# Attention with a state, then a GELU layer: two transposes moved in the start-up of a one-core kernel

## The chip, the cores and the metric

The kernel runs on one core of a Trainium2 chip. The metric is the device time of one execution in microseconds (us); the median of several executions counts. A core has the engines TensorE (PE in the profile; PEld are its weight loads), VectorE (DVE), ScalarE (ACT) and GpSimd (POOL), and SyncE (SP), which here only issues DMAs. Each engine works through its own list of instructions in order and waits on semaphores for the others.

## What is computed

For each of 8 batches and 8 heads, x (512 x 64) and a small state (32 x 64) attend to each other; the results of all heads, put side by side, go through a layer with an exact GELU:

```python
scores = scale * np.matmul(x, state.transpose(0, 1, 3, 2))
a = np.exp(scores - scores.max(-1, keepdims=True))
a /= a.sum(-1, keepdims=True) + 1e-09
xread = np.matmul(a, state)                    # 512 rows a batch
scores2 = scale * np.matmul(state, x.transpose(0, 1, 3, 2))
a2 = softmax(scores2)                          # written out in the same way
sread = np.matmul(a2, x)                       # 32 rows a batch
y = concat([xread, sread], axis=2)             # 4352 rows of 512, heads side by side
h = y @ w_in                                   # 512 x 2048
g = 0.5 * h * (1.0 + erf(h / sqrt(2)))
return g @ w_out                               # 2048 x 512
```

## The kernel before

The order of all instructions is written out by hand. It works by batches. For batch b:

- `load_x` (L115) fetches x by a GpSimd DMA into one of two `xb` buffers. `rearr` (L221) copies it on GpSimd into `x4`, from which `xtr_dma` (L276) makes the transposed `xT` by a DMA transpose on SyncE's queue; batch 1 is transposed on TensorE instead (`xtr`). `rearr_ones` (L230) makes a second copy `xo` of the same x, with a column of ones; for batches 2 and up it runs on GpSimd (L235). `xo` is read by `sread` (L379) alone, the product for the 32 state rows.
- `scores` (L323) multiplies xT by the state and takes the exponential on ScalarE in two halves. `norm` (L345) does on VectorE, for each half, a sum (L351), a reciprocal (L353) and a scaling (L354), which gives A, the tile `a`.
- A must be transposed to A^T (`AT`). Batch 1 does this with `atr` (L361): eight TensorE transposes into two PSUM tiles `aT_ps` and two VectorE copies. Batches 2 and up use `atr_dma` (L371), a DMA transpose on SyncE's queue.
- The state times w_in gives P, in four chunks of 512 columns: `p_mm` makes two PSUM tiles, `p_copy` casts one on ScalarE (L433) and one on VectorE (L434). `burst` makes several chunks in one run; `pmat` makes one. In P the state and the first layer are folded together, so that `M(k)` (`mm1`, L478) makes one block of 128 of the 2048 hidden columns of a batch by two matmuls of A^T with P, and a GELU on ScalarE (L492). `M(16, 17)` are blocks 0 and 1 of batch 1.
- The second layer of batch 0 runs in units `mm2_m(0, m)` (L520): four matmuls that add hidden block m to all four row tiles of the output. From `U(12)` on, units run by row tile (`mm2`, L505). Later batches use sums of quarter matrices (`g_sum`, `X`), for which `w_sums` (L547) prepares sums of w_out on VectorE.

PSUM has two groups of buffers. `ps_f` is a ring of four that `ftile` gives out in program order; each of its tiles takes the buffer that the fourth tile before it had, and waits for that one's reader. `hp`, `p_ps`, `aT_ps`, `srT`, `pt` and `sr` go through this ring. `otile` gives out four others, which hold the running outputs.

A GpSimd instruction that copies one column into the tile `hold` (128 x 1) is used three times further on to make GpSimd's list wait: it reads a block of g, so that it, and the load behind it, can't start before the GELU of that block.

The order around the first part of the change, batch 0's second layer and batch 1's start, is the lines L1032 to L1045. Around the second part it is L1063 to L1090: the hold and load of batch 4, `rearr(3)`, `xtr_dma(3)`, `rearr_ones(3)`, batch 2's scores and norm, the sums of w_out, `atr_dma(2)` and `pmat(2, 3)`. After it comes the loop over batches 2 to 7, whose first product is `M(32, 33)` with batch 2's A^T.

Of the kernel before, what the change touches and what calls it, by code (L numbers as in the profile page):

```python
# [17 lines left out]
def kernel(  # L18
# [8 lines left out]
    nc = tc.nc  # L27
# [27 lines left out]
    def otile(shape, name, at=None):  # L55
        if at is None:
            at = turn[0] % 4
            turn[0] += 1
        return ps_o.tile(shape, FP32, name=name, tag=f"o{at}")
# [19 lines left out]
    hold = persist.tile([128, 1], BF16, name="hold")  # L79
# [124 lines left out]
    atts = {}  # L204
# [25 lines left out]
    def rearr_ones(b):  # L230
        A = atts[b]
        eng = nc.vector if b < 2 else nc.gpsimd
        src = xbs[b].rearrange("p (t c) (j d) -> p t c j d", t=2, d=D)
        for t in range(2):
            eng.tensor_copy(  # L235
                out=A.xo[:, :, :, 2 + 64 * t:66 + 64 * t].rearrange("p j c d -> p c j d"),
                in_=src[:, t],
            )
# [37 lines left out]
    def xtr_dma(b):  # L276
        A = atts[b]
        nc.sync.dma_start_transpose(
            out=A.xT.rearrange("p j c n -> p (j c) n"),
            in_=A.x4.rearrange("p j c n -> p (j c n)"),  # L280
        )
# [79 lines left out]
    def atr(b, ts=(0, 1)):  # L361
        A = atts[b]
        if 0 in ts:
            A.AT = att.tile([128, SJ, 2, 128], BF16, name="AT", tag="AT")
        for t in ts:
            ps = ps_f.tile([128, SJ, 128], BF16, name="aT_ps", tag="f")
            for j in range(SJ):
                nc.tensor.transpose(ps[:, j, :], A.a[:, 2 * j + t, :], ident)
            nc.vector.tensor_copy(out=A.AT[:, :, t, :], in_=ps)

    def atr_dma(b):  # L371
        A = atts[b]
        A.AT = att.tile([128, SJ, 2, 128], BF16, name="AT", tag="AT")
        nc.sync.dma_start_transpose(
            out=A.AT.rearrange("p j t n -> p (j t) n"), in_=A.a
        )


    def sread(b):  # L379
        A = atts[b]  # L380
        A.sr = ftile([128, 2, 65], "sr")
        for t in range(2):
            for j in range(SJ):
                for c in range(HC):
                    nc.tensor.matmul(  # L385
                        A.sr[32 * c:32 * c + 32, t, :],
                        lhsT=A.e[:, 2 * j + t, 32 * c:32 * c + 32],
                        rhs=A.xo[:, j, c, 1 + 65 * t:66 + 65 * t],
                        start=(j == 0),
                        stop=(j == SJ - 1),  # L390
                    )

    def sread_out(b):
        A = atts[b]
        A.srm = att.tile([128, 2, D], BF16, name="srm", tag="srm")
        flat = A.sr.rearrange("q t d -> q (t d)")
        inv = att.tile([128, 2], FP32, name="inv", tag="inv")
        nc.vector.reciprocal(out=inv, in_=flat[:, 0:130:129])
        nc.vector.tensor_tensor(
            out=A.srm,  # L400
            in0=flat[:, 1:129].rearrange("q (t d) -> q t d", t=2),
            in1=inv[:, :].to_broadcast((128, 2, D)),
            op=ALU.mult,
        )
# [11 lines left out]
    def p_mm(b, f, tiles):  # L416
        if b not in Ps:
            Ps[b] = att.tile([128, 2, d_ff], BF16, name="P", tag="P")
        ps = [tiles([128, 512], "p_ps") for t in range(2)]
        for c in range(HC):  # L420
            for t in range(2):
                nc.tensor.matmul(  # L422
                    ps[t][32 * c:32 * c + 32, :],
                    lhsT=sbd[64 * t:64 * t + 64, b, c, 32 * t:32 * t + 32],
                    rhs=w_in_bf[64 * t:64 * t + 64, c, f * 512:(f + 1) * 512],
                    start=True,
                    stop=True,
                )
        return ps

    def p_copy(b, f, ps):
        dst = Ps[b][:, :, f * 512:(f + 1) * 512]
        nc.scalar.copy(out=dst[:, 0, :], in_=ps[0])  # L433
        nc.vector.tensor_copy(out=dst[:, 1, :], in_=ps[1])  # L434
# [7 lines left out]
    def burst(chunks, b_read=None):  # L442
        done = []
        first = len(chunks) < 4 and b_read is not None
        if first:
            sread(b_read)
        for i, (b, f) in enumerate(chunks):
            done.append((b, f, p_mm(b, f, ftile if i < 2 else otile)))
        for x in done[:2]:
            p_copy(*x)  # L450
        if b_read is not None and not first:
            sread(b_read)
        for x in done[2:3]:
            p_copy(*x)
        if b_read is not None:
            sread_out(b_read)
        for x in done[3:]:
            p_copy(*x)
# [21 lines left out]
    def mm1(b, m):  # L480
        if m == 0:
            gs[b] = gpool.tile([128, MC, S], BF16, name="g", tag="g")
        hp = ps_f.tile([128, S], FP32, name="hp", tag="f")
        for t in range(2):
            nc.tensor.matmul(  # L485
                hp,
                lhsT=Ps[b][:, t, m * 128:(m + 1) * 128],
                rhs=atts[b].AT[:, :, t, :],
                start=(t == 0),
                stop=(t == 1),  # L490
            )
        nc.scalar.activation(out=gs[b][:, m, :], in_=hp, func=AF.Gelu)  # L492
# [29 lines left out]
    def mm2_m(b, m):  # L522
        for j in range(SJ):
            if m == 0:
                ops[b, j] = otile([128, d_model], "op")
            nc.tensor.matmul(  # L526
                ops[b, j],
                lhsT=gs[b][:, m, j * 128:(j + 1) * 128],
                rhs=w_out_bf[:, m, :],
                start=(m == 0),  # L530
                stop=(m == MC - 1),
            )
# [364 lines left out]
    def M(*ms):  # L897
        for m in ms:
            mm1(m // MC, m % MC)

    def U(*us):
        for u in us:
            mm2(u // 16, u % 16 // 4, u % 4)
# [129 lines left out]
    mm2_m(0, 7)  # L1033
    M(8, 9)
    M(10, 11)
    atr(1)
    mm2_m(0, 8)
    M(16, 17)
    mm2_m(0, 9)
    burst([(0, 3), (1, 1)])  # L1040
    mm2_m(0, 10)
    M(12, 13)
    srt(1)
    M(14, 15)
# [21 lines left out]
    begin(3)  # L1066
    rearr(3)
    xtr_dma(3)
    rearr_ones(3)
    M(22, 23)  # L1070
    scores(2, 0)
    scores(2, 1)
# [9 lines left out]
    w_sums(2)  # L1082
    U(22)
    atr_dma(2)
    M(30, 31)
    U(23)
    pmat(2, 3)
# [121 lines left out]
```

## Time and profile before

| | us |
|---|---|
| median of 6 runs | 205.44 (205.32 to 206.47) |
| the profiled execution: its own time | 206.47 |
| the profiled execution: span from first to last instruction | 204.7 |
| busy: TensorE, VectorE, ScalarE, GpSimd | 198.5, 149.8, 134.7, 65.7 |
| idle ScalarE in front of the GELUs L492 | 29.7 |
| median landing of a DMA transpose AT, of xT | 4.4, 4.4 |

The profile is of one execution; its times count from the first instruction. A line of the timeline has the start, the duration of a group of equal instructions that follow each other, the engine and the source line, the operation with what it writes and reads, and in brackets the idle time before it and what ended it. A matmul of 512 columns is shown with 379 ns, but the next one starts 215 ns after it: matmuls overlap, and their starts tell more than their ends. For a DMA the duration is that of its issue; the time to landing is given apart.

### The profile page before, as it was taken

To read this page: it belongs to the slowest core of one execution; us is meant where nothing else is said; L and a number is where in the kernel's file an instruction comes from. 1 tells how busy PE (TensorE), PEld (TensorE's weight loads), DVE (VectorE), ACT (ScalarE), POOL (GpSimd) and SP (SyncE) were. 2 spreads that over 40 slices of the span, in tenths; PEclk is the share of its full clock that TensorE was granted. 3 is DMA by queue.
4 is the path that set the end of the run, shared out by engine and by line. 5 is a ranking of instruction groups with operands and counts; after the bars stand their busy time and mean duration, and the time that the engine had idled before them with its cause. 6 is when DMAs were issued, how large, how long until landed. Compare 5 with 4: busy or idle time off the path is not lost.

```text
span 204.7 us, 4793 instructions
## 1 busy us (share of the span) xinstructions
PE 198.5 (97%) x1991; PEld 128.5 (63%) x1991; DVE 149.8 (73%) x246; ACT 134.7 (66%) x238; POOL 65.7 (32%) x73
## 2 busy tenths in 40 slices
PE   7889999999999999999999999999999999999994
PEld 2443544444344567766876677657776787878893
DVE  2943873684875778977897787768778988895883
ACT  3775677379795869666966788487847666864120
POOL 8992710728060306271625702240220002200000
PEclk9999999999999999999999999999999999999999
DMA  6999999679647906743393503390109101030125
GB/s 200 193 180 200 205 197 194 116 225 129 132 46 158 244 17 85 157 146 81 44 188 93 140 3 95 91 179 0 54 0 183 25 3 51 3 154 0 54 99 159
DMA packets 40325, 23.14 MB, mean 113 GB/s; under 512 B 21872, under 2 KB 38384, under 8 KB 40304
## 3 DMA queue, kind: packets, MB, share of 16 engines
q0 software_dynamic: 14000, 8.10, 28.8%
q1 hardware_dynamic: 25616, 14.36, 27.9%
q10 hardware_dynamic: 688, 0.39, 0.6%
q8 instruction: 15, 0.25, 0.5%
q14 instruction: 6, 0.05, 0.1%
HBM read 17.30 MB, written 8.91 MB: 128 GB/s over the span
## 4 chain that ended last, share of the span: by engine, by line
PE 90%; DMA 4%; POOL 2%; ACT 1%; DVE 0%; issue 0%; POOLq 0%
PE xp L581 34%; PE hp L485 25%; PE op L511 8%; PE op L526 5%; PE p_ps L422 4%; PE sp L787 3%; PE rp L853 3%; DMA w_in_bf<-in_moe_w_in_dram 3%; PE xp L692 2%; DMA AT<-a 2%; PE pt L331 2%; PE sr L385 1%; POOL w_in_bf L105 1%; PE hp L997 1%; POOL sbd L95 1%; ACT L492 1%
## 5 line engine op out<-in xcount | busy, mean ns | idle before, releaser
L492 ACT ACTIVATE g<-hp 128x512 bf16<-128x512 f32 x124 | 67.0, 602 | 29.7 <-PE hp L485 24.3
L485 PE MATMUL hp<-AT,P 128*128 128x512 bf16 x248 | 63.3, 379 | 0.3 <-DMA AT<-a 0.3
L581 PEld LDWEIGHTS <-gsum 128*128 128x128 bf16 x448 | 43.3, 98 | 10.4 <-issue 1.9
L575 DVE TENSOR_TENSOR gsum<-g 128x2048 bf16<-128x2048 bf16 x30 | 38.7, 1306 | 0.1
L485 PEld LDWEIGHTS <-P 128*128 128x128 bf16 x248 | 22.8, 98 | 22.2 <-issue 2.1
L581 PE MATMUL xp<-ws,gsum 128*128 128x256 bf16 x256 | 30.6, 273 | 0.0
L434 DVE CAST P<-p_ps 128x512 bf16<-128x512 f32 x31 | 20.0, 685 | 6.8 <-PE p_ps L422 6.7
L581 PE MATMUL xp<-ws,g 128*128 128x256 bf16 x192 | 22.9, 273 | 0.0
L581 PE MATMUL xp<-w_out_bf,gsum 128*128 128x256 bf16 x192 | 22.8, 273 | 0.0
L581 PEld LDWEIGHTS <-g 128*128 128x128 bf16 x192 | 18.7, 98 | 4.1
L433 ACT CAST P<-p_ps 128x512 bf16<-128x512 f32 x31 | 16.8, 597 | 6.6 <-PE p_ps L422 5.7
L635 POOL TENSOR_TENSOR u<-s,oh 128x512 f32<-128x512 f32 x5 | 6.6, 1314 | 41.1 <-ACT oh L632 41.1
L511 PE MATMUL op<-w_out_bf,g 128*128 128x512 bf16 x80 | 19.7, 379 | 0.0
L235 POOL COPY xo<-xb 128x1024 bf16<-128x1024 bf16 x12 | 14.5, 1237 | 12.8 <-PE sr L385 12.8
L225 POOL COPY x<-xb 128x1024 bf16<-128x1024 bf16 x12 | 12.1, 1043 | 8.6 <-DMA xb<-in_x_dram 8.6
L600 POOL TENSOR_TENSOR v<-q,oh 128x512 f32<-128x512 f32 x5 | 7.1, 1429 | 20.4 <-ACT oh L637 20.4
L511 PEld LDWEIGHTS <-g 128*128 128x128 bf16 x80 | 7.6, 98 | 9.3 <-issue 0.8
L351 DVE TENSOR_REDUCE cs<-e 128x16 f32<-128x512 bf16 x14 | 9.5, 678 | 4.3 <-ACT e L338 4.3
L526 PE MATMUL op<-w_out_bf,g 128*128 128x512 bf16 x48 | 11.8, 380 | 0.0
L354 DVE TENSOR_TENSOR a<-e,ics 128x512 bf16<-128x512 bf16 x14 | 10.6, 756 | 0.5
L422 PE MATMUL p_ps<-w_in_bf,sbd 64*32 64x512 bf16 x248 | 10.1, 382 | 0.0
L412 DVE COPY XSR<-srT 128x128 bf16<-128x128 bf16 x8 | 5.7, 758 | 5.8 <-PE srT L409 5.8
(126 smaller groups left out, 235.8 us busy)
## 6 DMA issues: line engine op xcount, KB each, us to landing
xb<-in_x_dram POOLq DMA_DIRECT2D x7, 512.0 KB, 6.2
out_dram<-oh SPq DMA_DIRECT2D x13, 256.0 KB, 2.4
out_dram<-osb SPq DMA_DIRECT2D x10, 256.0 KB, 2.9
out_dram<-oh SPq DMA_DIRECT2D x5, 512.0 KB, 2.8
w_out_bf<-in_moe_w_out_dram POOLq DMA_DIRECT2D x8, 256.0 KB, 9.7
w_in_bf<-in_moe_w_in_dram POOLq DMA_DIRECT2D x6, 256.0 KB, 10.2
x0f<-in_x_dram SPq DMA_DIRECT2D x3, 256.0 KB, 4.0
w_in_bf<-in_moe_w_in_dram POOLq DMA_DIRECT2D x4, 128.0 KB, 4.7
```

The source lines that it names most:

```text
L225: nc.gpsimd.tensor_copy(out=A.x4[:, :, :, 64 * t:64 * t + 64].rearrange("p j c d -> p c j d"), in_=src[:, t],)
L235: eng.tensor_copy(out=A.xo[:, :, :, 2 + 64 * t:66 + 64 * t].rearrange("p j c d -> p c j d"), in_=src[:, t],)
L354: nc.vector.tensor_tensor(out=A.a[:, :, hs].rearrange("p g (c n) -> p g c n", n=NS), in0=e4, in1=ics[:, :, :].to_broadcast((128, G, 2, NS) ...
L422: nc.tensor.matmul(ps[t][32 * c:32 * c + 32, :], lhsT=sbd[64 * t:64 * t + 64, b, c, 32 * t:32 * t + 32], rhs=w_in_bf[64 * t:64 * t + 64, c ...
L433: nc.scalar.copy(out=dst[:, 0, :], in_=ps[0])
L434: nc.vector.tensor_copy(out=dst[:, 1, :], in_=ps[1])
L485: nc.tensor.matmul(hp, lhsT=Ps[b][:, t, m * 128:(m + 1) * 128], rhs=atts[b].AT[:, :, t, :], start=(t == 0), stop=(t == 1),)
L492: nc.scalar.activation(out=gs[b][:, m, :], in_=hp, func=AF.Gelu)
L511: nc.tensor.matmul(ps, lhsT=gs[b][:, m, j * 128:(j + 1) * 128], rhs=w_out_bf[:, m, :], start=(m == 0), stop=(m == MC - 1),)
L526: nc.tensor.matmul(ops[b, j], lhsT=gs[b][:, m, j * 128:(j + 1) * 128], rhs=w_out_bf[:, m, :], start=(m == 0), stop=(m == MC - 1),)
L575: nc.vector.tensor_tensor(out=t, in0=g_q(b, h0, k0), in1=g_q(b, h1, k1), op=op)
L581: nc.tensor.matmul(ps[:, j - js[0], :], lhsT=lhs[:, m, 128 * j:128 * j + 128], rhs=rhs[:, m, :], start=(first and j == js[0] and m == 0), ...
```

## The change

The first part permutes calls of the hand-written order. `mm2_m(0, 8)` moves ahead of `atr(1)`; the run of the chunks (1, 1) and (0, 3) moves ahead of `M(16, 17)`, with its two chunks in the other order. The second part takes `rearr_ones(3)` from behind `xtr_dma(3)` to behind `atr_dma(2)`, and puts a new GpSimd copy into `hold` in front of it that reads a column of the second half of batch 2's A, so that it waits for `norm(2, 1)`.

```diff
     mm2_m(0, 7)
     M(8, 9)
     M(10, 11)
+    mm2_m(0, 8)
     atr(1)
-    mm2_m(0, 8)
+    mm2_m(0, 9)
+    burst([(1, 1), (0, 3)])
+    mm2_m(0, 10)
     M(16, 17)
-    mm2_m(0, 9)
-    burst([(0, 3), (1, 1)])
-    mm2_m(0, 10)
     M(12, 13)
     srt(1)
     M(14, 15)
@@
     begin(3)
     rearr(3)
     xtr_dma(3)
-    rearr_ones(3)
     M(22, 23)
     scores(2, 0)
     scores(2, 1)
@@
     w_sums(2)
     U(22)
     atr_dma(2)
+    nc.gpsimd.tensor_copy(out=hold, in_=atts[2].a[:, 0, 64:65])
+    rearr_ones(3)
     M(30, 31)
     U(23)
     pmat(2, 3)
```

The number of instructions of each engine stays as it was, but for one more on GpSimd.

## The prediction

> **What bounds the kernel now.** I read the page first, then the list of what TensorE waits for, then the timeline of TensorE around each wait, then that of the engine it waits for. On the page TensorE is busy for 97% of the span and holds 90% of the chain that ended last, so only an interval in which TensorE itself stands still can be won or lost. The list of its waits (who, for whom: total us, times, longest) leaves two after the start-up:
>
> ```profile
> PE 198.5 (97%) x1991; PEld 128.5 (63%) x1991; DVE 149.8 (73%) x246; ACT 134.7 (66%) x238; POOL 65.7 (32%) x73
> ...
> PE aT_ps L368 <- ACT g L492: 0.3, 1, 0.3
> PE hp L485 <- DMA AT<-a: 0.3, 1, 0.3
> ```
>
> The timeline shows where they lie (start us, duration us, engine, line, operation; in brackets the idle time before it):
>
> ```profile
> 27.64 1.03 PE L485 MATMUL hp<-AT,P 128*128 128x512 bf16 x4
> 29.01 0.62 PE L368 MATMUL aT_ps<-ident,a 128*128 128x128 bf16 x8 [0.35 <-ACT g L492]
> 29.47 1.03 PE L526 MATMUL op<-w_out_bf,g 128*128 128x512 bf16 x4
> 30.33 1.03 PE L485 MATMUL hp<-AT,P 128*128 128x512 bf16 x4
> ...
> 29.01 0.45 PEld L368 LDWEIGHTS <-a 128*128 128x128 bf16 x8 [0.84 <-DVE a L354]
> ...
> 28.27 0.69 DVE L354 TENSOR_TENSOR a<-e,ics 128x512 bf16<-128x512 bf16 x1
> ```
>
> Matmul ends are modelled and overlap the next start, so I go by starts: four matmuls of 512 columns take 0.86 (29.47 to 30.33), 0.215 each. The last L485 starts at 27.64 + 3 x 0.215 = 28.29; unhindered, the next would start at 28.50; it starts at 29.01. The loss is 0.51, not the bracket's 0.35. The bracket names ScalarE, the weight load VectorE: L354 ends at 28.96, and the load starts 0.05 later. VectorE decides.
>
> The second place is the first use of batch 2's A^T, and its cause is four microseconds earlier:
>
> ```profile
> 55.07 0.41 PE L422 MATMUL p_ps<-w_in_bf,sbd 64*32 64x512 bf16 x8
> 55.76 1.04 PE L485 MATMUL hp<-AT,P 128*128 128x512 bf16 x4 [0.28 <-DMA AT<-a]
> ...
> 49.68 1.07 DVE L354 TENSOR_TENSOR a<-e,ics 128x512 bf16<-128x512 bf16 x1
> 50.67 0.67 DVE L351 TENSOR_REDUCE cs<-e 128x16 f32<-128x512 bf16 x1
> 51.37 0.25 DVE L353 RECIPROCAL ics<-cs 128x16 f32<-128x16 f32 x1
> 51.66 0.69 DVE L354 TENSOR_TENSOR a<-e,ics 128x512 bf16<-128x512 bf16 x1
> 52.27 2.35 DVE L547 TENSOR_TENSOR ws<-w_out_bf 128x2048 bf16<-128x2048 bf16 x2
> 55.58 0.69 DVE L434 CAST P<-p_ps 128x512 bf16<-128x512 f32 x1 [0.95 <-PE p_ps L422]
> ...
> 48.17 2.02 POOL L235 COPY xo<-xb 128x1024 bf16<-128x1024 bf16 x2
> 57.19 0.26 POOL L1131 COPY hold<-g 128x1 bf16<-128x1 bf16 x1 [7.00 <-ACT g L492]
> ...
> 52.41 1.23 SPq L374 DMA_TRANSPOSE AT<-a  x1
> ```
>
> The earlier such step, eight p_ps matmuls at 25.56 and the next at 25.90, takes 0.34, so L485 could start at 55.41 and loses 0.35. The same scaling L354 takes 1.07 while GpSimd's L235 runs (to 50.19) and 0.69 without it.
>
> **The change, part 1.** Nothing is added; PE instructions are permuted. The unit mm2_m(0, 8) now stands before atr(1). It reads block 8 of g, whose GELU is the first of the four at 27.93 and lasts 0.60, so it ends at 28.53; with the 0.05 above its weights load at 28.58. The first matmul starts at 28.58 instead of 28.50, and A (28.96) is long there when atr(1) follows at 28.58 + 0.86 = 29.44. Everything behind comes 29.01 - 28.58 = 0.43 earlier. The other inputs of the moved work are in place: the last transfer of w_in's fourth chunk, issued at 19.54 and 10.0 to landing, is there at 29.5; the run that reads it moves from 32.15 to about 30.85.
>
> What the permutation can give back lies in ps_f's ring of four buffers. M(16, 17) now follows the run, so six GELUs queue where two and then four did. By the old intervals (mm2_m(0, 9) at 31.20, run at 32.15, next unit at 32.71) the new starts are mm2_m(0, 9) 29.90, run 30.85, mm2_m(0, 10) 31.41, M(16) 32.28, M(12) 33.14, M(14) 34.07 behind srt(1), M(15) 34.50. A GELU starts 0.63 after its block's first matmul (30.33 to 30.96) and in a queue every 0.49 (six take 3.04 at 50.44, the last 0.60), so 16, 17 and 12 end at 33.51, 34.00 and 34.49. M(14) takes 17's buffer, free at 34.05: in time. M(15) takes 12's, free at 34.54: 0.04 late. The run's own buffers are those of M(10) and M(11) (GELUs over by 30.00) and of the two transposes, copied out by about 30.7. The fourth chunk's casts are over by some 32.7, before M(12). Unit U(12) needs GELU 15 (about 36.0) at its fourth matmul, some 36.5. Part 1 is worth 0.43 - 0.04 = 0.39, between 0.30, if the ring costs three times as much, and 0.43.
>
> **The change, part 2.** One instruction is added: a GpSimd copy of 128x1 that waits for VectorE's second L354. Rows for such a copy run from 0.26 (57.19) to 0.83 (44.58, beside an L547). Behind it on GpSimd stand the two L235 copies, then the copy L1131 with the load of batch 5 and the rearranging of batch 4; these wait for a GELU until 57.19 anyway, after 7.00 idle. No DMA is issued by the moved step, and SyncE's order is unchanged. L235's output is read by sread(3), behind the sread at 68.42.
>
> With GpSimd silent, the first L354 takes 0.69: the chain of six ends 0.38 earlier, at 51.97, and the transpose is issued at 52.03 instead of 52.41. The profile gives it 3.3 us to landing, so it lands 0.38 earlier, by 55.37 against a need at 55.41, and the whole 0.35 goes. SyncE's preceding transpose, issued at 48.27 and held 3.11, has left its queue at 51.38.
>
> The copies now collide with w_sums(1) and (2), the two L547. How much is bounded from the rows: a 128x2048 tensor_tensor took 2.52 at 78.70 where GpSimd's copies of 2.02 had begun at 78.11, and 1.22 alone; conversely an L235 took 1.92 instead of 1.04 when such an operation had begun first. At worst one operation follows the other: 51.9 + 1.22 + 0.26 + 2.03 + 1.22 = 56.6 for VectorE, at best 54.3. The cast at 55.58 would slip about a microsecond, to end at 57.3. It hands its bank to the second half of scores(3), at 58.36 + 0.24 less 0.35, so 0.9 of cover is left. Next, w_sums(3) and (4) would end at 59.6, a half microsecond behind norm(3)'s due time; the 2.16 that VectorE idles before 63.35 absorb that. GpSimd ends at 56.6 at the latest, before the shifted L1131. I take nothing for the collision; without these covers it would cost that half microsecond to one microsecond.
>
> Here a rule of the Trainium skill speaks against the change: SBUF — State Buffer, section SBUF: two separate sides, says that VectorE and GpSimd share a port pair as an exclusive lock for a whole instruction, so that moving the copy only moves the block. The rows at 49.68, 78.70 and 90.16 agree. By the rule the two engines' work behind the scaling is done serially, which is the 56.6 worked out above; by a sharing of bandwidth it would be less, and the sum is the same by both as long as the cover holds. The same section says that a DMA is not slowed by a compute operation, which would keep the transpose at 3.3 beside GpSimd's copies; no row settles it, because the transposes that ran beside L235 also had output stores ahead of them.
>
> That is the open cost. The six transposes L374 took 3.3, 5.0, 3.7, 3.7, 5.2 and 5.6. The first is this one, with no store ahead of it in its queue; the next four had GpSimd's copies beside them. Ends for part 2 are thus 0.35 (3.3 again) and a loss (5.6). The nearest row is its own 3.3, since no store is moved ahead of it; I grant it half of 0.1 for the tail of the xT transpose that it now follows more closely and take 0.30.
>
> **Sum.** 0.39 + 0.30 = 0.69. The profiled execution took 206.47, 1.77 around a span of 204.7; it would take 205.78. It is the highest of the six runs, 1.03 over their median; what exceeds the median is not in question here, so I carry the saving over: 205.44 - 0.69 = 204.75, or -0.34%. What this kernel's measurement can tell from no change is about 0.3%, that is 0.62 us, so even the full gain stands only just beyond it.
>
> **Rivals.**
> Only part 1 counts: GpSimd's copies beside the transpose cost it what the 3.7 rows show, 0.4 more, and it lands at 55.73, where it did. 205.44 - 0.39 = 205.05. For it: two rows. Against: their stores.
> It does not do what it says: part 1's gain goes into the ring, since GELUs queue six deep and M(14), at 34.07 against 34.05, has no margin, and part 2's into the landing: about 205.3. Against: the paces used are rows of this trace.
> Slower: the transpose takes 5.0 to 5.6 as three of the six did, here for company on its way. At 5.3 it lands at 57.33; TensorE would stand 1.92 instead of 0.35, and with part 1 the time is 205.44 + 1.57 - 0.39 = 206.6. It decides from 52.03 + t - 55.41 = 0.74, t = 4.1 us; from t = 4.7 it is over 0.3% slower. Against: those three had stores just ahead.
>
> **How the numbers follow.** Chances: the forecast 0.68, of which 0.62 beyond 0.3% and 0.06 short of it (its own range 204.55 to 204.9); only part 1, 0.15; nothing, 0.07; slower, 0.10. Faster 0.62, same 0.06 + 0.15 + 0.07 = 0.28, slower 0.10. The likeliest time is 204.75. The range takes in part 1 alone and nearly the third case, 204.5 to 205.3, and leaves out the slow case and the ends.
>
> **What would show it.** Right: no idle time before L368, which starts after an L526; M(15) at most 0.1 late; the L354 near 49.3 at 0.69; L374's landing before TensorE needs it and no bracket before its L485; L547 longer than 2.35 with the cast late, and nobody waiting for it. Wrong: TensorE idle before M(14) or M(15), a landing over 3.6, or scores(3) waiting for VectorE's cast.

## The result, and the profile after

| | before | after |
|---|---|---|
| median, us (runs) | 205.43 (51) | 204.94 (25) |
| ratio, 95% interval | | 0.997 (0.9958 to 0.9982) |
| the profiled execution: own time, span | 206.47, 204.7 | 205.48, 203.7 |

The change makes the kernel faster by 0.3%, and the interval leaves no change out. The medians lie 0.49 us apart, the two profiled executions 0.99.

The list of TensorE's waits after the change holds nothing behind the start-up (who, for whom: total us, times, longest):

```profile
PE warm_ps L150 <- DVE warm L92: 1.2, 1, 1.2
PE xT_ps L257 <- DVE x0b L243: 0.8, 1, 0.8
```

Both waits are over by 8.1 us. The timeline of TensorE at the two places, first batch 1's transposes and the blocks behind the run:

```profile
26.57 1.89 PE L485 MATMUL hp<-AT,P 128*128 128x512 bf16 x8
28.38 1.04 PE L526 MATMUL op<-w_out_bf,g 128*128 128x512 bf16 x4
29.25 0.61 PE L368 MATMUL aT_ps<-ident,a 128*128 128x128 bf16 x8
29.70 1.03 PE L526 MATMUL op<-w_out_bf,g 128*128 128x512 bf16 x4
30.65 0.62 PE L422 MATMUL p_ps<-w_in_bf,sbd 64*32 64x512 bf16 x16
31.21 1.04 PE L526 MATMUL op<-w_out_bf,g 128*128 128x512 bf16 x4
32.08 1.89 PE L485 MATMUL hp<-AT,P 128*128 128x512 bf16 x8
33.81 0.22 PE L409 MATMUL srT<-ident,srm 128*128 128x128 bf16 x1
33.87 1.07 PE L485 MATMUL hp<-AT,P 128*128 128x512 bf16 x4
```

The brackets are gone: the unit L526 stands where TensorE stood. From the last L485 of the first line (26.57 + 7 x 0.216 = 28.08) to the L526 it takes 0.30 instead of 0.216, so 0.08 of the old 0.51 is left. The last line is M(14, 15): four matmuls in 1.07 where 1.03 is the rule, which is the 0.04 that M(15) waits for a buffer.

At the second place VectorE, GpSimd and TensorE now look like this:

```profile
49.08 0.69 DVE L354 TENSOR_TENSOR a<-e,ics 128x512 bf16<-128x512 bf16 x1
...
51.30 2.35 DVE L547 TENSOR_TENSOR ws<-w_out_bf 128x2048 bf16<-128x2048 bf16 x2
54.98 0.69 DVE L434 CAST P<-p_ps 128x512 bf16<-128x512 f32 x1 [1.33 <-PE p_ps L422]
...
51.51 1.06 POOL L1084 COPY hold<-a 128x1 bf16<-128x1 bf16 x1 [3.87 <-DVE a L354]
52.50 3.04 POOL L235 COPY xo<-xb 128x1024 bf16<-128x1024 bf16 x2
56.24 0.61 POOL L1132 COPY hold<-g 128x1 bf16<-128x1 bf16 x1 [0.70 <-ACT g L492]
...
54.47 0.41 PE L422 MATMUL p_ps<-w_in_bf,sbd 64*32 64x512 bf16 x8
54.81 1.04 PE L485 MATMUL hp<-AT,P 128*128 128x512 bf16 x4
```

The scaling takes 0.69 and L485 follows the eight p_ps matmuls after 0.34, without a wait. The collision that the held copies were to bring is there, but GpSimd pays for it: its copies take 3.04 instead of 2.02 and its small copy 1.06, while both L547 take 2.35 as before and the cast waits only for TensorE. What GpSimd has left in front of its next instruction is 0.70 of the old 7.00.

### The profile page after: what moved, and what is told of

It reads as the page before. It is cut to its first block, busy times and chain, and to the rows that moved or that the text cites. A ratio compares the mean times of both kernels' runs of the same rounds, so it can differ in the third digit from the quotient of the medians.

```text
span 203.7 us, 4795 instructions
## 1 busy us (share of the span) xinstructions
PE 198.3 (97%) x1991; PEld 128.7 (63%) x1991; DVE 149.3 (73%) x246; ACT 134.6 (66%) x238; POOL 68.4 (34%) x74
## 4 chain that ended last, share of the span: by engine, by line
PE 94%; DMA 3%; DVE 1%; SPq 0%; issue 0%; ACT 0%
PE xp L581 35%; PE hp L485 27%; PE op L511 9%; PE op L526 5%; PE p_ps L422 4%; PE sp L787 3%; PE rp L853 3%; DMA x0f<-in_x_dram 3%; PE xp L692 2%; PE pt L331 2%; PE sr L385 1%; PE hp L997 1%; PE warm_ps L150 1%; PE xT_ps L271 0%; SPq L91 0%; PE aT_ps L368 0%
## 5 line engine op out<-in xcount | busy, mean ns | idle before, releaser
L485 PE MATMUL hp<-AT,P 128*128 128x512 bf16 x248 | 63.2, 379 | 0.0
L485 PEld LDWEIGHTS <-P 128*128 128x128 bf16 x248 | 22.8, 98 | 21.9 <-issue 2.2
L235 POOL COPY xo<-xb 128x1024 bf16<-128x1024 bf16 x12 | 15.5, 1321 | 12.7 <-PE sr L385 12.7
L511 PE MATMUL op<-w_out_bf,g 128*128 128x512 bf16 x80 | 19.7, 379 | 0.0
L511 PEld LDWEIGHTS <-g 128*128 128x128 bf16 x80 | 7.6, 98 | 9.3 <-issue 0.8
L526 PE MATMUL op<-w_out_bf,g 128*128 128x512 bf16 x48 | 11.8, 380 | 0.0
L354 DVE TENSOR_TENSOR a<-e,ics 128x512 bf16<-128x512 bf16 x14 | 10.3, 735 | 0.5
L422 PE MATMUL p_ps<-w_in_bf,sbd 64*32 64x512 bf16 x248 | 10.1, 382 | 0.0
```

The source lines that it names most:

```text
L235: eng.tensor_copy(out=A.xo[:, :, :, 2 + 64 * t:66 + 64 * t].rearrange("p j c d -> p c j d"), in_=src[:, t],)
L354: nc.vector.tensor_tensor(out=A.a[:, :, hs].rearrange("p g (c n) -> p g c n", n=NS), in0=e4, in1=ics[:, :, :].to_broadcast((128, G, 2, NS) ...
L422: nc.tensor.matmul(ps[t][32 * c:32 * c + 32, :], lhsT=sbd[64 * t:64 * t + 64, b, c, 32 * t:32 * t + 32], rhs=w_in_bf[64 * t:64 * t + 64, c ...
L485: nc.tensor.matmul(hp, lhsT=Ps[b][:, t, m * 128:(m + 1) * 128], rhs=atts[b].AT[:, :, t, :], start=(t == 0), stop=(t == 1),)
L511: nc.tensor.matmul(ps, lhsT=gs[b][:, m, j * 128:(j + 1) * 128], rhs=w_out_bf[:, m, :], start=(m == 0), stop=(m == MC - 1),)
L526: nc.tensor.matmul(ops[b, j], lhsT=gs[b][:, m, j * 128:(j + 1) * 128], rhs=w_out_bf[:, m, :], start=(m == 0), stop=(m == MC - 1),)
```

## The experiments

All spans of TensorE's work are compared by two intervals, which the start-up doesn't enter: from the start of the second sread (L385) to U(12) (the first L511), where part 1 lies, and from the first matmul of batch 2's scores to that of batch 3's (L331), where part 2 lies. In the two traces at hand they are 11.03 and 12.49 before, 10.64 and 12.13 after: 0.39 + 0.36 = 0.75, against 0.49 between the medians. The first four runs ask what becomes of the rest.

**The kernel before again.** No edit.

> The kernel before once more, with a second profile. The two traces at hand differ by 0.74 us between TensorE's first GELU blocks of batch 0 and the loop, the medians by 0.49. Theory A (both stalls are there in every execution, the rest is spread of the start-up): ratio 1.000 within 0.002; TensorE again stands before L368 (start 0.51 late) and before the first L485 with batch 2's A^T (0.35 late). Theory B (the profiled execution had a longer second stall than most): that stall is 0.1 or less, and the first one is as before.

Ratio 0.9989 (0.9974 to 1.0003), median 205.36. The first stall is as it was, the second is not:

```profile
28.05 0.62 PE L368 MATMUL aT_ps<-ident,a 128*128 128x128 bf16 x8 [0.35 <-ACT g L492]
...
54.10 0.41 PE L422 MATMUL p_ps<-w_in_bf,sbd 64*32 64x512 bf16 x8
54.57 1.04 PE L485 MATMUL hp<-AT,P 128*128 128x512 bf16 x4
```

From L422 to L485 it takes 0.47, 0.13 over the 0.34 that the step needs, where the first trace had 0.69. The chain in front is unchanged (L354 again takes 1.07); the transpose took 3.07 us to landing instead of 3.30. So theory B comes nearer: the first profiled execution had a longer second stall than this one, although 0.13 is left, a little over what B allowed.

**Part 1 alone.** The change without its second part:

```diff
     xtr_dma(3)
+    rearr_ones(3)
@@
     atr_dma(2)
-    nc.gpsimd.tensor_copy(out=hold, in_=atts[2].a[:, 0, 64:65])
-    rearr_ones(3)
```

> Only the permuted TensorE order; GpSimd's second copy of batch 3's x where it was. Theory A: 0.39 us less than before, ratio 0.998, no wait before L368, M(15) 0.04 late, and the stall before batch 2's first L485 unchanged at 0.35. Rival (the ring of four buffers gives it back): ratio 1.000, TensorE idle before M(14) or M(15) for 0.2 or more.

Ratio 0.9968 (0.9954 to 0.9982), median 204.89. The first interval is 10.64, 0.39 shorter, as expected; no wait before L368. The ratio came out lower than the 0.998 expected, but its interval still holds it. The second interval is 12.39, so the stall was 0.26 this time (landing 3.20).

**Part 2 alone.** The change with the old TensorE order:

```diff
     M(10, 11)
-    mm2_m(0, 8)
     atr(1)
-    mm2_m(0, 9)
-    burst([(1, 1), (0, 3)])
-    mm2_m(0, 10)
+    mm2_m(0, 8)
     M(16, 17)
+    mm2_m(0, 9)
+    burst([(0, 3), (1, 1)])
+    mm2_m(0, 10)
```

> Only the held copy; the TensorE order as before. Theory A: 0.35 us less, ratio 0.998; the first L354 of batch 2 takes 0.69 instead of 1.07, the transpose lands 0.38 earlier against TensorE's list, the wait before L368 stays. Rival (that stall is a matter of the one profile, or the landing eats it): ratio 1.000.

Ratio 0.9991 (0.9973 to 1.0009), median 205.23, 0.13 under the run of the kernel before beside it. The mechanism is as told (L354 at 0.69, second interval 12.13, first 11.03), the size is not: against the 12.26 of the kernel before on the same chip part 2 is worth 0.13, and the times can't tell that from nothing.

**The changed kernel again.** No edit.

> The changed kernel once more on the same chip as the three others. Theory A: the sum of the two parts, 0.74 us less, ratio 0.9964. Theory B: 0.4 to 0.5 less, ratio 0.998, and part 2 alone near 1.000.

Ratio 0.9968 (0.9943 to 0.9992), median 204.88, the same as part 1 alone. Its intervals are 10.64 and 12.13. In the trace both stalls are gone, as theory A has it. The medians have what theory B gave (0.48 below the run of the kernel before beside it), which fits with 0.13 instead of 0.36 as the second stall of that run; the ratio's interval alone leaves both theories open.

**Only the unit.** Is the rest of part 1's order needed?

```diff
     mm2_m(0, 8)
     atr(1)
+    M(16, 17)
     mm2_m(0, 9)
-    burst([(1, 1), (0, 3)])
+    burst([(0, 3), (1, 1)])
     mm2_m(0, 10)
-    M(16, 17)
```

> Of part 1 only mm2_m(0, 8) ahead of atr(1); M(16, 17) directly behind atr(1), the run in its old place and order; part 2 as in the change. The interval between TensorE's second sread and U(12) was 11.03 us before and 10.64 with part 1. Theory: the gain of 0.43 stands, but M(16) now meets the two VectorE copies of A^T, the first over 0.86 and the second 1.19 after the first transpose, and loses 0.45 + 0.11: interval 11.16. Rival (the unit alone brings the gain, the rest of the order is idle): 10.60.

The first interval is 11.17, 0.14 longer than before the change; ratio 0.9993 (0.9969 to 1.0016). The timeline of TensorE and of VectorE:

```profile
28.48 0.61 PE L368 MATMUL aT_ps<-ident,a 128*128 128x128 bf16 x8
29.39 1.14 PE L485 MATMUL hp<-AT,P 128*128 128x512 bf16 x4 [0.30 <-DVE AT L369]
...
28.90 0.76 DVE L369 COPY AT<-aT_ps 128x512 bf16<-128x512 bf16 x2 [0.92 <-PE aT_ps L368]
```

The unit that fills the wait before the transposes was the cover of the wait behind them. Without another, M(16) stands for the copies of A^T, and the four matmuls take 1.14 for the second copy. So the rest of the permutation brings no gain of its own; it keeps the 0.43 from being lost again.

**The blocks before the run.** The other order that has a unit behind the transposes:

```diff
     mm2_m(0, 9)
-    burst([(1, 1), (0, 3)])
-    mm2_m(0, 10)
     M(16, 17)
+    burst([(0, 3), (1, 1)])
+    mm2_m(0, 10)
     M(12, 13)
```

> Part 1 with mm2_m(0, 8), atr(1), mm2_m(0, 9), but M(16, 17) ahead of the run, which keeps its old order; part 2 as in the change. Theory (the ring of four buffers is what orders these calls): the run's second chunk takes the buffers of M(16) and M(17), whose GELUs end 1.2 and 1.7 after M(16) starts; it comes 0.60 late: interval 11.20. Rival (the order of run and blocks is worth only the 0.04 of M(15)): 10.60.

The first interval is 11.19, ratio 0.9988 (0.9966 to 1.001). The run of the two chunks takes twice its time:

```profile
29.89 1.03 PE L485 MATMUL hp<-AT,P 128*128 128x512 bf16 x4
30.85 1.22 PE L422 MATMUL p_ps<-w_in_bf,sbd 64*32 64x512 bf16 x16
32.00 1.04 PE L526 MATMUL op<-w_out_bf,g 128*128 128x512 bf16 x3
```

From 30.85 to the next unit it takes 1.15 where 0.56 is the rule: its second chunk waits for the GELUs of M(16) and M(17), as the ring has it. In the kernel before a unit stood between the blocks and the run; in the change the run stands ahead of the blocks.

**Held behind the first half.** The same copies between VectorE's two scalings:

```diff
-    nc.gpsimd.tensor_copy(out=hold, in_=atts[2].a[:, 0, 64:65])
+    nc.gpsimd.tensor_copy(out=hold, in_=atts[2].a[:, 0, 0:1])
```

> The change, with the added GpSimd copy reading the first half of batch 2's A, so that the copies start between VectorE's two scalings. The interval between the scores of batches 2 and 3 was 12.13 with part 2, and 12.49, 12.26 and 12.39 without. Theory (the two engines exclude each other for whole instructions, and GpSimd's two copies follow without a break): the second L354 takes about 2.1 instead of 0.69, A is complete 1.4 later, the transpose comes 1.1 late: interval 13.2, time about 0.5 over before. Rival (sharing, or VectorE gets in between the copies): the L354 takes 1.1 at most, interval 12.1 to 12.5.

The loss that the theory gave did not come. The second interval is 12.15 and the ratio 0.9969 (0.9947 to 0.9991):

```profile
49.99 0.92 DVE L354 TENSOR_TENSOR a<-e,ics 128x512 bf16<-128x512 bf16 x1
50.84 2.05 DVE L547 TENSOR_TENSOR ws<-w_out_bf 128x2048 bf16<-128x2048 bf16 x1
...
49.20 0.19 POOL L1084 COPY hold<-a 128x1 bf16<-128x1 bf16 x1 [2.26 <-DVE a L354]
49.33 2.49 POOL L235 COPY xo<-xb 128x1024 bf16<-128x1024 bf16 x2
...
50.31 1.51 POOL L235 COPY xo<-xb 128x1024 bf16<-128x1024 bf16 x1
```

The second scaling waits only until GpSimd's first copy is over (about 50.3) and then goes ahead of the second, which takes 1.51 for it; VectorE's next operation then waits for that copy and takes 2.05. Here the engines take turns by instruction. Each of the three blocked operations is longer by what was left of the other engine's operation, less 0.14 to 0.15 (0.38, 0.60 and 0.98 were left; the delays are 0.23, 0.47 and 0.83), so one waits for the other rather than sharing with it. The price was 0.23 on the scaling, and the transpose came 0.02 late at most.

**Held late.** The copies behind the cast of the fourth chunk, so that GpSimd is silent while the transpose is on its way:

```diff
     atr_dma(2)
-    nc.gpsimd.tensor_copy(out=hold, in_=atts[2].a[:, 0, 64:65])
-    rearr_ones(3)
     M(30, 31)
     U(23)
     pmat(2, 3)
+    nc.gpsimd.tensor_copy(out=hold, in_=Ps[2][:, 1, 1536:1537])
+    rearr_ones(3)
```

> The change, with the added GpSimd copy reading batch 2's fourth chunk of P and standing behind pmat(2, 3), so that GpSimd is silent while the transpose is on its way. Theory (GpSimd's copies do not slow the transpose, which took 3.07 to 3.15 beside them): landing 3.05 to 3.3, interval between the scores 12.13, ratio 0.997 as the change; GpSimd's list behind runs 3 us later and nobody waits. Rival (the copies cost the transpose some tenths): landing 2.9 or less.

The landing is 3.09, the second interval 12.13, the ratio 0.9961 (0.9941 to 0.9982). With GpSimd's copies beside it the transpose took 3.05 to 3.15 in six profiles, without them 3.09 here: they cost it nothing that shows. That agrees with the sentence weighed in the prediction (the Trainium skill, SBUF — State Buffer, section SBUF: two separate sides), that a compute operation does not slow a DMA. GpSimd's load of batch 5 is issued at 59.38; counted from the first L997 (11.12 here, 12.10 in the changed kernel, where the load is at 56.79) that is 3.6 later, and the intervals behind are the same.

**The second stall twice more.** No edit for the first, part 1 alone for the second.

> The kernel before a third time, for its second stall alone. In three profiles without part 2 the transpose of batch 2's A took 3.30, 3.07 and 3.20 us to landing and the interval between the scores of batches 2 and 3 was 12.49, 12.26 and 12.39; with part 2 it is 12.13. Theory: the stall is the landing less 2.94, so it is 0.1 to 0.4 here too. Rival (the landing has nothing to do with it): interval and landing do not move together.

> Part 1 alone again, for the same two numbers: interval between sread and U(12) 10.64; landing 3.05 to 3.35 and interval between the scores 9.19 more than the landing, that is 12.24 to 12.54.

The times, of one execution each, are 205.40 and 204.98. The landings are 3.08 and 3.08, the intervals of the scores 12.27 and 12.27; the first interval is 11.03 and 10.64. Both lie on the rule that the expectations wrote down, though both at its short end: how the stall grows with the landing still rests on the three profiles that the rule was read from. The table has all twelve profiles:

| kernel | part 2 | landing, us | interval of the scores, us | stall, us |
|---|---|---|---|---|
| before | no | 3.30 | 12.49 | 0.36 |
| before again | no | 3.07 | 12.26 | 0.13 |
| before, third | no | 3.08 | 12.27 | 0.14 |
| part 1 alone | no | 3.20 | 12.39 | 0.26 |
| part 1, second | no | 3.08 | 12.27 | 0.14 |
| part 2 alone | yes | 3.07 | 12.13 | 0 |
| after | yes | 3.08 | 12.13 | 0 |
| after again | yes | 3.15 | 12.13 | 0 |
| the unit only | yes | 3.05 | 12.13 | 0 |
| the blocks before the run | yes | 3.15 | 12.13 | 0 |
| held behind the first half | half | 3.10 | 12.15 | 0.02 |
| held late | yes | 3.09 | 12.13 | 0 |

Without part 2 the stall is the landing less 2.94, to 0.01. With it the transpose starts 0.38 earlier, so landings up to 3.32 would be covered; the longest seen with it is 3.15.

## Why the prediction was right, and what was off

- The time was forecast at 204.75 and came to 204.94; the forecast saving of 0.69 compares with 0.49 between the medians, and the range held the time. The forecast that it would be just beyond 0.3% was too sharp: the ratio's interval reaches from 0.2% to 0.4%.
- Part 1, term 0.39: the interval is 0.39 shorter in every profile that has the new order. The 0.51 from starts, not the 0.35 in the bracket, was the loss to count from, and VectorE, not the ScalarE that the bracket names, ended it. M(15)'s 0.04 is in the trace, and the two other orders cost what the steps for the A^T copies and for the ring give (11.17 and 11.19, expected 11.16 and 11.20).
- Part 2, term 0.30: mis-sized. The scaling (0.69), the earlier transpose (0.38) and the missing wait came as told, but "the whole 0.35 goes" took the landing of one execution, 3.3, for the rule. The sum then carried that saving over to the median, as if nothing of the 1.03 by which the profiled execution lay above it were in question; some 0.2 of it was this stall. The 3.3 was the longest of all profiles; in the five without part 2 the stall was 0.13 to 0.36, its median 0.14, its mean 0.21. With 0.39 that makes 0.53 by the median and 0.60 by the mean, against 0.49 between the medians of the times; the ratio's interval, 0.37 to 0.86 us, holds both. So the time came near the forecast by part 1 and by the width of the range, not by the size of this term, which is about twice too large. In the times part 2 does not show: the medians of part 1 alone (204.89) and of the whole change (204.88, 204.94) lie within 0.06 of each other.
- The half of 0.1 granted for the tail of the xT transpose was not paid: with the whole of part 2, xT landed 0.91 to 1.38 us after the issue of A's transpose (0.53 to 0.79 without), and A's took 3.05 to 3.15 all the same. What made it 3.30 and 3.20 in two profiles stays open.
- The collision with w_sums: the 56.6 was bounded rightly, the payer was not. VectorE's first L547 had begun (51.30) when GpSimd's small copy came (51.51), and VectorE stayed ahead; the cast did not slip at all. Taking nothing for it was right, for a better reason than the covers named.
- "Only part 1 counts" got 0.15 and is the rival that came nearest: the time can't tell the change from its first part. Its mechanism is not what happened: GpSimd's copies did not hold up the transpose.
- "It does not do what it says" fell: neither the ring nor the landing took the gains. The slow rival had no sign: no transpose of batch 2 took more than 3.30 in any profile. That output stores make the later ones long was not tried.

## What to carry to other kernels

Work that is moved to fill a wait may have covered another one: when a unit is moved ahead of a stall, look at once for what stands behind it bare, and count the buffers of the ring for the new order. A stall that ends with a DMA's landing should be sized from several executions; one profile can show its longest case. Read the loss from the starts of the pipelined engine and who ended it from the weight load, not from the bracket alone.

## What the runs showed of the hardware

The length of the start-up differs between executions. Of the 1.21 us between the first two profiled executions of the kernel before (206.47 and 205.26), 0.97 lies ahead of the first L997, which starts at 12.31 and 11.34; in one of part 1 it starts at 11.12. From the scores of batch 3 to the last matmul all twelve profiles of the table agree within 0.02. The two profiled executions at the head of this document differ by 0.99 us, of which 0.21 is start-up and 0.75 the two places.

VectorE and GpSimd took turns by instruction when both had work queued in the held-behind-the-first-half run. In the trace of before, at 78.70, a VectorE sum of 128x2048 stayed blocked over both of GpSimd's copies instead (2.52 against 1.22 alone). What decides between the two is open. The size of a block is the same in both: the sum at 78.70 met 1.43 us of copies and took 1.30 longer, 0.13 less, and the scaling at 49.68 in the kernel before met 0.51 and took 0.38 longer, 0.14 less.
